# Rearranging the first pairs of batch 1 and the hand-over to batch 2 in a fused attention and expert kernel

## The chip, the cores and the metric

The kernel runs on one core of a Trainium2 chip. The metric is the device time of one execution in microseconds (us): the median of several runs. The profile is one execution, recorded by the hardware profiler. The engines are TensorE (PE in the profile: matrix products; PEld: its weight loads), VectorE (DVE), ScalarE (ACT), GpSimd (POOL) and SyncE (SP, which only issues transfers). [...]

## What is computed

Attention over 8 batches of 8 heads, 576 tokens and head width 64, in which a token sees the tokens within 32 places of it, and 8 "global" tokens see and are seen by all. Its output, as 4608 rows of 512, then goes through an expert layer with a squared Relu:

```python
scores = scale * q @ k.T                    # scale = 1/8
mask   = |pos_i - pos_j| <= 32  or  i global  or  j global
attn   = softmax(where(mask, scores, -1e9))
x      = (attn @ v)  as rows (batch, token), columns (head, width)   # 4608 x 512
h      = x @ w_in                           # 512 x 2048
out    = relu(h)**2 @ w_out                 # 2048 x 512, float32
```

## The kernel before

The attention of a batch is done in four pairs of heads (`hp`), the expert layer in nine chunks of 512 rows. The expert work is cut into units that stand in a list `queue`; `take(n)` emits the next n of them. The attention of one pair is laid between such units, so that TensorE has something to do while ScalarE and VectorE work on the pair.

```python
def take(n):
    for _ in range(min(n, len(queue))):
        fn, a = queue.pop(0)
        fn(*a)

def mm1_half(u, half, ...):        # chunk 0, first product, in two halves of 256 rows: 8 units each
    ...                            # 8 matmuls into one of three "mm" banks, then:
    rl = sbt("rl", [P, TC], FP16, bufs=3)...
    if u % 8 == 6:
        nc.vector.tensor_scalar(out=rl, in0=ph, ..., op0=ALU.max)
    else:
        nc.scalar.activation(out=rl, in_=ph, func=AF.Relu)
    nc.vector.tensor_tensor(out=gts[0][...], in0=rl, in1=rl, op=ALU.mult)
```

The other units are `mm1` (a column block of a later chunk: four matmuls of 512 columns, Relu, squaring) and `mm2` (four of the sixteen matmuls of 512 columns that make 128 output rows; the last one also copies the rows out of PSUM and stores them).

Batches 0 and 1 come in by token and are transposed on TensorE. Keys are copied out of PSUM by VectorE, queries by ScalarE:

```python
def tr_k(i, op=None, tail=None, last=None, tag="mm"):
    op = op or dve.tensor_copy
    tk, gl = transposed("k", i, tag)              # TensorE
    op(out=kt[:, 0:4, 8:P]..., in_=tk[:, 0:80]...)
    (tail or op)(out=kt[:, 4, 8 : 8 + KN[4]]..., in_=tk[:, 80:96])
    (last or op)(out=kt[:, :, 0:NG], in_=gl...)   # the global keys
```

`tr_q` does the same for queries in two copies. The rows of the global tokens' values are put ahead of each of the five key tiles:

```python
def v_globals(b, rows):
    dve.tensor_copy(out=gv16, in_=rows)
    for x in range(NT):                           # NT = 5
        dve.tensor_copy(out=vb[b][0:NG, x, 0 : 2 * H : 2], in_=gv16)
```

The start of the kernel:

```python
cast_tokens(dve.tensor_copy, "k", 0)
cast_tokens(dve.tensor_copy, "q", 0)
transposes0(0)                                    # tr_k(0), then tr_q(0)
cast_tokens(dve.tensor_copy, "k", 1)
cast_tokens(act.copy, "q", 1)
mask_natural(0)                                   # VectorE
keep_warm(SCHED["w3"])                            # filler: matmuls of a constant tile
tr_k(1, tail=act.copy, last=act.copy)
mg = mask_globals_matmul(0)                       # TensorE, reads the mask
keep_warm(SCHED["w4"])
tr_q(1, act.copy)
mask_globals(mg, 0)
...
```

From the end of batch 0 to batch 2. `scatter` writes the global tokens' outputs into their columns of `xT`, in eight copies on VectorE; chunk 0's second half reads them.

```python
tr_k(NHP, tag="tr")                               # NHP = 4: the first pair of batch 1
tr_q(NHP, tag="mm", op=act.copy)
scatter(0, 1)
v_globals(1, grow["v"][:, 0])
take(99)                                          # what is left of chunk 0's first half
queue += units[1] + units[2]                      # 8 + 16 units

def unit(i, n, nxt=None):
    scs = [scores(i, half, pair_tag[half], WIN2) for half in range(2)]   # TensorE
    et = [weights(half, scs[half], WIN2) for half in range(2)]           # exp on ScalarE, mask on VectorE
    take(n[0])
    if nxt:
        tr_k(nxt, tag="tr", tail=act.copy)
        tr_q(nxt, tag="mm", op=act.copy)
    for half in range(2):
        acc = outputs(i, half, et[half], ...)                            # TensorE
        finish_outputs(i, half, acc, ...)          # ln and exp on ScalarE, scaling on VectorE
        if half == 0:
            take(n[1])
    if i % NHP == NHP - 1:
        scatter(i // NHP)
    take(n[2])

for hp in range(NHP):
    unit(NHP + hp, SCHED["b1"][hp], NHP + hp + 1 if hp + 1 < NHP else None)   # (2, 1, 3) each
    if hp == 0:
        next_in_place()         # VectorE casts batch 2's global rows of k, q, v
        globals_to_scratch(2)   # SyncE: those rows of k and q into a scratch in DRAM
        pool.tensor_copy(out=pin[0:1], ...)
        tokens_to_scratch(2)    # GpSimd: the tokens of k and q into it, cast on the way
        transposes(2)           # SyncE: DMA transposes, scratch -> kb, qb
        vb[2] = vb[0]
        values(2)               # GpSimd: values, cast on the way
        value_globals(2)        # SyncE: global rows of the values
    if hp == 2:
        clear_ones(dve.memset, vb[0])
        index_base()
gather_index()
gather(0)
for b in range(2, B):
    queue += units[b + 1]
    for hp in range(NHP):
        unit(NHP * b + hp, ((2, 1, 4), (3, 1, 4), (2, 1, 5), (2, 1, 6))[hp])
        ...                     # at hp == 0: the same transfers for batch b + 1
    take(99)
queue += units[B + 1] + units[B + 2]
take(999)
```

Of the kernel before, what the change touches and what calls it, by code (L numbers as in the profile page):

```python
# [9 lines left out]
FP16 = mybir.dt.float16  # L10
# [8 lines left out]
NT = 5  # L19
# [20 lines left out]
)  # L40
W2 = 440
MB = (0, 456)
SCHED = dict(w5=2, w6=1, w7=2, wa=4, wb=3, wc=3, w0=6, w1=5, w2=2, w3=4, w4=0, w=4, h0=1, h1=1, h2=3, h3=0, b1=((2, 1, 3), (2, 1, 3), (2, 1, 3), (2, 1, 3)))
ONES = 2.0**-7 * (1.0 + 15360.0 / 2**23)


# [1 line left out]
def kernel(  # L48
# [29 lines left out]
    def sbt(name, shape, dtype, bufs=1, tag=None):  # L78
        return sb.tile(shape, dtype, name=name, tag=(tag or name), bufs=bufs)
# [260 lines left out]
    def store_rows(nm, b):  # L340
        gscr[(nm, b)] = dram.tile([NG, H * D], FP16, name=f"gscr_{nm}{b}")
        nc.sync.dma_start(
            out=gscr[(nm, b)].rearrange("g (h d) -> (g h) d", d=D), in_=gathered(nm, b)
        )
# [29 lines left out]
    def globals_to_scratch(b):  # L374
        for nm in "kq":
            rows, n, pitch, off = {"k": (KW, NT, P, 0), "q": (QW, 4, GRP, GTOK)}[nm]
            if (nm, b % 2) not in scr:
                scr[(nm, b % 2)] = dram.tile([rows, H * D], FP16, name=f"scr_{nm}{b % 2}")
                if nm == "k":
                    nc.sync.dma_start(  # L380
                        out=scr[("k", b % 2)][(NT - 1) * P + 8 + KN[-1] : KW],
                        in_=idle[0 : P - 8 - KN[-1]],
                    )
            t = scr[(nm, b % 2)]
            dst = t.rearrange("(x r) (h d) -> x r h d", x=n, d=D)[:, off : off + NG]
            if b == 2:
                nc.sync.dma_start(
                    out=dst.rearrange("x g h d -> g x (h d)"),
                    in_=g16s[nm].rearrange("g h d -> g (h d)").unsqueeze(1).to_broadcast(
                        (NG, n, H * D)  # L390
                    ),
                )
                continue
            nc.sync.dma_start(
                out=dst.rearrange("x g h d -> (g h) x d"),
                in_=gathered(nm, b).unsqueeze(1).to_broadcast((NG * H, n, D)),
            )
        if b > 2:
            store_rows("v", b)

    def tokens_to_scratch(b):
        for nm in "kq":
# [36 lines left out]

    gv16 = sbt("gv16", [NG, H, D], FP16)  # L440

    def v_globals(b, rows):
        dve.tensor_copy(out=gv16, in_=rows)
        for x in range(NT):
            dve.tensor_copy(out=vb[b][0:NG, x, 0 : 2 * H : 2], in_=gv16)

    def transposed(nm, i, tag):
        b, hp = divmod(i, NHP)
# [23 lines left out]
                    )  # L472
        return tr[:, 0:S].rearrange("p (j q) -> p q j", j=TJ), gl

    def tr_k(i, op=None, tail=None, last=None, tag="mm"):
        op = op or dve.tensor_copy
        tk, gl = transposed("k", i, tag)
        kt = kts[i % NHP]
        op(
            out=kt[:, 0:4, 8:P].rearrange("p t (q j) -> p t q j", j=TJ),  # L480
            in_=tk[:, 0:80].rearrange("p (t q) j -> p t q j", t=4),
        )
        (tail or op)(
            out=kt[:, 4, 8 : 8 + KN[4]].rearrange("p (q j) -> p q j", j=TJ), in_=tk[:, 80:96]
        )
        (last or op)(out=kt[:, :, 0:NG], in_=gl.unsqueeze(1).to_broadcast((P, NT, NG)))

    def tr_q(i, op=None, tag="mm"):
        op = op or dve.tensor_copy
        tq, gl = transposed("q", i, tag)  # L490
        q4 = qts[i % NHP].rearrange("p (g x) -> p g x", x=GRP)
        op(
            out=q4[:, :, 0:GTOK].rearrange("p g (q j) -> p g q j", j=TJ),
            in_=tq.rearrange("p (g q) j -> p g q j", g=4),
        )
        op(out=q4[:, :, GTOK:GRP], in_=gl.unsqueeze(1).to_broadcast((P, 4, NG)))
# [8 lines left out]
    def mm1(c, u):  # L505
        if c not in gts:
            gts[c] = sbt("gt", [P, NFF, TC], FP16, bufs=2)
        ph = expert_bank() if c else pst("mm", [P, 512])
        for t in range(NDM):
            nc.tensor.matmul(  # L510
                ph, w_in[:, t, u * P : (u + 1) * P], xT[:, t, XOFF + c * TC : XOFF + (c + 1) * TC],
                start=(t == 0), stop=(t == NDM - 1),
            )
        rl = sbt("rl", [P, TC], FP16, bufs=3)
        nc.scalar.activation(out=rl, in_=ph, func=AF.Relu)  # L515
        nc.vector.tensor_tensor(out=gts[c][:, u, :], in0=rl, in1=rl, op=ALU.mult)  # L516

# [2 lines left out]
    def mm1_half(u, half, tiles=range(NDM)):  # L520

        if 0 not in gts:
            gts[0] = sbt("gt", [P, NFF, TC], FP16, bufs=2)
        if 0 in tiles:
            ph_now[u] = pst("mm", [P, 2, 256])
        ph = ph_now[u]
        for j in range(2):
            for t in tiles:
                nc.tensor.matmul(
                    ph[:, j], w_in[:, t, (u + j) * P : (u + j + 1) * P],  # L530
                    xT[:, t, half * (256 + XOFF) : half * (256 + XOFF) + 256],
                    start=(t == 0 and j == 0), stop=(t == NDM - 1), skip_group_check=True,
                )
        if NDM - 1 not in tiles:
            return
        rl = sbt("rl", [P, TC], FP16, bufs=3).rearrange("p (j x) -> p j x", j=2)
        if u % 8 == 6:
            nc.vector.tensor_scalar(out=rl, in0=ph, scalar1=0.0, scalar2=None, op0=ALU.max)
        else:
            nc.scalar.activation(out=rl, in_=ph, func=AF.Relu)  # L540
        nc.vector.tensor_tensor(  # L541
            out=gts[0][:, u : u + 2, half * 256 : half * 256 + 256], in0=rl, in1=rl, op=ALU.mult
        )
# [192 lines left out]
    wv = moe_w_in.rearrange("(t p) f -> p t f", p=P)  # L736
    wo = moe_w_out.rearrange("(t p) m -> p t m", p=P)

    def transposes0(hp):
        tr_k(hp, tail=act.copy, last=act.copy)  # L740
        tr_q(hp, act.copy)

    keep_warm(SCHED["w0"])
    gb = indices()
# [2 lines left out]
    constants()  # L747
    one_hots(gb)
    cast_tokens(dve.tensor_copy, "k", 0)
    cast_tokens(dve.tensor_copy, "q", 0)  # L750
    transposes0(0)
    cast_tokens(dve.tensor_copy, "k", 1)
    cast_tokens(act.copy, "q", 1)
    mask_natural(0)
    keep_warm(SCHED["w3"])
    tr_k(1, tail=act.copy, last=act.copy)
    mg = mask_globals_matmul(0)
    keep_warm(SCHED["w4"])
    tr_q(1, act.copy)
    mask_globals(mg, 0)  # L760
    ets = {}

# [29 lines left out]
        fetch_values(1, x)  # L792
    for j in range(4):
        pool.dma_start(out=w_out[:, ts(j, 4), :], in_=wo[:, ts(j, 4), :])
    v_globals(0, gv0)
    half0(2)
    keep_warm(SCHED["w6"])
    half0(3)
# [36 lines left out]
    tr_k(NHP, tag="tr")  # L835
    tr_q(NHP, tag="mm", op=act.copy)
    scatter(0, 1)
    v_globals(1, grow["v"][:, 0])
    take(99)
    queue += units[1] + units[2]  # L840

    def unit(i, n, nxt=None):
        scs = [scores(i, half, pair_tag[half], WIN2) for half in range(2)]
        et = [weights(half, scs[half], WIN2) for half in range(2)]
        take(n[0])
        if nxt:
            tr_k(nxt, tag="tr", tail=act.copy)
            tr_q(nxt, tag="mm", op=act.copy)
        for half in range(2):
            acc = outputs(i, half, et[half], pair_tag[half], WIN2, columns=i < 2 * NHP)  # L850
            finish_outputs(i, half, acc, columns=i < 2 * NHP)
            if half == 0:
                take(n[1])
        if i % NHP == NHP - 1:
            scatter(i // NHP)
        take(n[2])

    for hp in range(NHP):
        unit(NHP + hp, SCHED["b1"][hp], NHP + hp + 1 if hp + 1 < NHP else None)
        if hp == 0:  # L860
            next_in_place()
            globals_to_scratch(2)
            pool.tensor_copy(out=pin[0:1], in_=xT[0:1, 0, XOFF + 256 : XOFF + 257])
            tokens_to_scratch(2)
            transposes(2)
            vb[2] = vb[0]
            values(2)
            value_globals(2)
        if hp == 2:
            clear_ones(dve.memset, vb[0])  # L870
            index_base()
    gather_index()
    gather(0)
    for b in range(2, B):
        queue += units[b + 1]
        for hp in range(NHP):
            unit(NHP * b + hp, ((2, 1, 4), (3, 1, 4), (2, 1, 5), (2, 1, 6))[hp])
            if b == 2 and hp:
                clear_ones(dve.memset, vb[1], range(2 * hp - 2, min(2 * hp, NT)))
            if hp == 0 and b + 1 < B:  # L880
                pool.tensor_copy(out=pin[0:1], in_=gsum[b][0:1, 0, 0, 0, 0:1])  # L881
                globals_to_scratch(b + 1)
                tokens_to_scratch(b + 1)
                transposes(b + 1)
                vb[b + 1] = vb[(b + 1) % 2]
                values(b + 1)
                value_globals(b + 1)
                if b in (2, 4):
                    gather(b // 2)
        take(99)  # L890
# [32 lines left out]
```

## Time and profile before

| what | value |
|---|---|
| time, median of 3 runs | 331.21 us (330.42 to 332.45) |
| span of the profiled execution | 329.3 us, granted TensorE clock 1.00 |
| TensorE busy | 316.9 us, 96% |
| VectorE busy | 231.1 us, 70% |
| ScalarE busy | 210.2 us, 64% |
| GpSimd busy | 106.5 us, 32% |
| TensorE, VectorE, ScalarE busy in the 10 us from 30 us | 7.98, 8.73, 7.10 us |
| the same, 40 to 50 us | 8.34, 8.46, 5.97 us |
| the same, 50 to 60 us | 9.59, 6.60, 5.50 us |
| the same, 60 to 70 us | 9.71, 8.36, 4.35 us |

"Busy" is the time in which an engine has an instruction running; TensorE's filler matmuls at the start count as busy too. A line of a timeline gives the start and the length of a group of like instructions in us, the engine, the line of the program, the operation, what it writes and reads, and in brackets how long the engine was idle before it and which instruction ended that. L529 are the matmuls of chunk 0's halves, L510 and L573 those of the later units, L458 the transposes, L613 the scores, L649 and L658 the outputs.

### The profile page before, as it was taken

What the parts mean: (1) busy time and instruction counts of PE and PEld (TensorE: products, weight loads), DVE (VectorE), ACT (ScalarE), POOL (GpSimd) and SP (SyncE); (2) the same over time, 40 slices, a digit from 0 to 9 for tenths busy, and PEclk for the clock granted to TensorE, in tenths of its full rate; (3) what the DMA queues carried; (4) which work ended last, traced back from release to release, by engine and by line L of the source; (5) the groups of instructions that cost most, each with busy time, mean ns of one, the idle gap of its engine ahead of it and who ended that gap; (6) DMA issues with size and microseconds to landing.
All of it is one profiled execution on the core that took longest, in us unless ns stands there. A gap on an engine that the chain in (4) does not pass through costs nothing.

```text
span 329.3 us, 6919 instructions
## 1 busy us (share of the span) xinstructions
PE 316.9 (96%) x2427; PEld 164.9 (50%) x2427; DVE 231.1 (70%) x684; ACT 210.2 (64%) x416; POOL 106.5 (32%) x138
## 2 busy tenths in 40 slices
PE   8889699999999999999999999999999999999996
PEld 3657574545554555455545554455454544444444
DVE  6896987788769775988588858885888584323421
ACT  2879574469954995499549954995499537404700
POOL 9734645019920770079207800680000000000000
PEclk9999999999999999999999999999999999999999
DMA  8999999949999999399959994999610001011012
GB/s 190 176 204 183 178 180 147 162 141 78 142 141 168 73 145 169 109 96 144 124 143 100 135 149 118 115 148 120 128 66 0 34 33 64 2 64 64 2 49 78
DMA packets 148356, 37.55 MB, mean 114 GB/s; under 512 B 136298, under 2 KB 143842, under 8 KB 148322
## 3 DMA queue, kind: packets, MB, share of 16 engines
q0 software_dynamic: 105168, 17.93, 77.1%
q1 hardware_dynamic: 43008, 19.05, 30.7%
q8 instruction: 19, 0.31, 0.4%
q14 instruction: 15, 0.12, 0.1%
q10 hardware_dynamic: 146, 0.13, 0.1%
HBM read 37.31 MB, written 17.05 MB: 165 GB/s over the span
## 4 chain that ended last, share of the span: by engine, by line
PE 78%; DVE 11%; ACT 5%; issue 2%; DMA 2%; SPq 2%; DVEq 0%
PE mm L573 25%; PE mm L510 25%; PE tr L510 9%; PE tr L573 6%; PE sc L658 3%; PE acc L658 3%; PE sc L613 2%; DVE xT L730 2%; ACT rec L682 2%; SPq L357 2%; ACT rec L681 2%; PE acc L613 2%; DMA grows<-in_k_dram 1%; DVE xT L711 1%; DVE gt L541 1%
## 5 line engine op out<-in xcount | busy, mean ns | idle before, releaser
L573 PE MATMUL mm<-w_out,gt 128*128 128x512 f16 x448 | 104.4, 379 | 0.0
L510 PE MATMUL mm<-xT,w_in 128*128 128x512 f16 x384 | 90.1, 379 | 0.8 <-DVE xT L730 0.8
L573 PEld LDWEIGHTS <-gt 128*128 128x128 f16 x560 | 52.5, 98 | 58.6
L510 PEld LDWEIGHTS <-w_in 128*128 128x128 f16 x512 | 47.5, 98 | 53.9 <-issue 1.0
L515 ACT ACTIVATE rl<-mm 128x512 f16<-128x512 f32 x96 | 54.9, 599 | 25.9 <-PE mm L510 25.3
L516 DVE TENSOR_TENSOR gt<-rl 128x512 f16<-128x512 f16 x128 | 52.0, 423 | 16.7 <-ACT rl L515 14.6
L622 ACT ACTIVATE et<-sc 128x880 f16<-128x880 f32 (+1 forms) x32 | 28.9, 902 | 44.7 <-PE sc L613 44.7
L625 DVE TENSOR_TENSOR et<-et,mask 128x880 f16<-128x880 f16 (+1 forms) x64 | 38.7, 613 | 22.4 <-ACT et L622 22.1
L113 POOL DMA_DIRECT2D vb<-in_v_dram x40 | 40.7, 1551 | 8.3 <-DMA w_in<-in_moe_w_in_dram 7.1
L510 PE MATMUL tr<-xT,w_in 128*128 128x512 f16 x128 | 33.0, 380 | 0.0
L550 DVE COPY ot<-mm 128x512 f32<-128x512 f32 (+1 forms) x29 | 19.7, 679 | 17.5 <-PE mm L573 15.8
L711 DVE TENSOR_TENSOR xT<-sc,rec 64x288 f16<-64x288 f32 (+1 forms) x55 | 25.0, 455 | 7.2 <-ACT rec L682 6.9
L682 ACT ACTIVATE rec<-rec 128x288 f32<-128x288 f32 x64 | 28.3, 443 | 2.0
L622 ACT ACTIVATE et<-acc 128x880 f16<-128x880 f32 (+1 forms) x32 | 29.0, 905 | 0.0
L658 PEld LDWEIGHTS <-vb 128*128 128x128 f16 x288 | 21.2, 98 | 12.9 <-issue 2.1
L711 DVE TENSOR_TENSOR xT<-acc,rec 64x288 f16<-64x288 f32 (+1 forms) x55 | 25.0, 455 | 3.7 <-ACT rec L682 0.9
L406 POOL DMA_DIRECT2D scr_k<-in_k_dram x30 | 26.5, 1084 | 2.5 <-issue 2.0
L406 POOL DMA_DIRECT2D scr_q<-in_q_dram x24 | 24.8, 1553 | 4.9 <-DMA w_out<-in_moe_w_out_dram 4.9
L681 ACT ACTIVATE rec<-sc 64x288 f32<-64x288 f32 (+1 forms) x55 | 22.4, 407 | 6.1 <-PE sc L658 4.2
L573 PE MATMUL tr<-w_out,gt 128*128 128x512 f16 x112 | 25.3, 379 | 0.0
L881 POOL COPY pin<-gsh 1x1 f32<-1x1 f32 x5 | 0.9, 185 | 70.9 <-DVE gsh L699 70.9
L681 ACT ACTIVATE rec<-acc 64x288 f32<-64x288 f32 (+1 forms) x55 | 22.2, 404 | 1.5 <-PE acc L649 0.6
(143 smaller groups left out, 302.1 us busy)
## 6 DMA issues: line engine op xcount, KB each, us to landing
out_dram<-ot SPq DMA_DIRECT2D x35, 256.0 KB
vb<-in_v_dram POOLq DMA_DIRECT2D x32, 120.0 KB, 10.7
scr_q<-in_q_dram POOLq DMA_DIRECT2D x24, 144.0 KB, 5.7
scr_k<-in_k_dram POOLq DMA_DIRECT2D x24, 120.0 KB, 4.6
w_in<-in_moe_w_in_dram POOLq DMA_DIRECT2D x4, 512.0 KB, 11.4
w_out<-in_moe_w_out_dram POOLq DMA_DIRECT2D x4, 512.0 KB, 12.5
natk<-in_k_dram POOLq DMA_DIRECT2D x3, 288.0 KB, 14.4
natq<-in_q_dram POOLq DMA_DIRECT2D x3, 288.0 KB, 15.1
```

The costliest lines, as they stand in the source:

```text
L113: pool.dma_start(out=vb[b][NG : NG + KN[x], x, 2 * hs.start : 2 * hs.stop : 2], in_=v[b, hs, x * KT : x * KT + KN[x]].rearrange("h s d -> ...
L406: pool.dma_start(out=scr[(nm, b % 2)][x * pitch + off : x * pitch + off + hi - lo].rearrange("s (h d) -> s h d", d=D), in_=src[nm][b, :, l ...
L510: nc.tensor.matmul(ph, w_in[:, t, u * P : (u + 1) * P], xT[:, t, XOFF + c * TC : XOFF + (c + 1) * TC], start=(t == 0), stop=(t == NDM - 1),)
L515: nc.scalar.activation(out=rl, in_=ph, func=AF.Relu)
L516: nc.vector.tensor_tensor(out=gts[c][:, u, :], in0=rl, in1=rl, op=ALU.mult)
L573: nc.tensor.matmul(po, gts[c][:, f, m * P : (m + 1) * P], w_out[:, f, :], start=(f == 0), stop=(f == NFF - 1),)
L622: act.activation(out=et[:, :, 0:W], in_=sc[:, :, 0:W], func=AF.Exp, bias=0.0, scale=scale)
L625: dve.tensor_tensor(out=et[:, :, 0:W], in0=et[:, :, 0:W], in1=mask[:, MB[half] : MB[half] + W].unsqueeze(1).to_broadcast((P, 2, W)), op=AL ...
L658: nc.tensor.matmul(banks[e][:, o : o + w], vtf[:, t, vo : vo + P], et[:, e, so : so + w], start=(n == 0), stop=(n == nw - 1), skip_group_c ...
L681: act.activation(out=rec[r], in_=av[xs][rs, :, 0:GTOK], func=AF.Ln)
L682: act.activation(out=rec, in_=rec, func=AF.Exp, scale=-1.0)
L711: dve.tensor_tensor(out=xT[r, hp, x0 : x0 + HS].rearrange("p (k x) -> p k x", k=2), in0=av[x][r, :, 0:GTOK], in1=rec[r], op=ALU.mult,)
```

## The change

The change spreads the work around the first pair of batch 1 over more engines, keeps an expert unit in hand for the places where TensorE has nothing else, and does the preparation of batch 2 in smaller pieces. Part by part:

1. **Start.** The first pair's queries are cast on ScalarE in place of VectorE. In both pairs the query copies come ahead of the key tails on ScalarE. The second pair's key transposes come after the mask's matmul.
2. **First pair of batch 1.** Of chunk 0's first half one unit is held back (`keep=1`) until the pair's scores are out, and the pair takes three units there in place of two. The value rows' cast goes to ScalarE, and of the five copies two; VectorE does three, after the pair's weights.
3. **Query copy ahead of key tail** in the other pairs of batch 1 too.
4. **Relu of chunk 0's halves.** Four `rl` buffers in place of three; VectorE does the Relu of units (0, 6), (1, 4) and (1, 12), where it did (0, 6), (0, 14), (1, 6) and (1, 14).
5. **Batch 2's rows.** The cast of its global rows, their way to the scratch, the transposes and the value rows come after the second pair of batch 1, where they came after the first. The token transfers and the values stay after the first. The scratch tensors are made there.
6. **Small VectorE work.** The ones of batch 2's values are set in two pieces, after the weights of the third and the fourth pair; the index arithmetic and the gather of later batches' rows go to the third pair.
7. **Units per pair.** Batch 1's last pair takes two at its end in place of three, so that one unit is left over for batch 2's first pair; the last batch takes one less in its third pair and one more after its scatter.

```diff
-SCHED = dict(..., h3=0, b1=((2, 1, 3), (2, 1, 3), (2, 1, 3), (2, 1, 3)))
+SCHED = dict(..., h3=0, keep=1, b1=((3, 1, 3), (2, 1, 3), (2, 1, 3), (2, 1, 2)), last=((2, 1, 4), (3, 1, 4), (2, 1, 4), (2, 1, 7)))
 ...
-    def v_globals(b, rows):
-        dve.tensor_copy(out=gv16, in_=rows)
-        for x in range(NT):
-            dve.tensor_copy(out=vb[b][0:NG, x, 0 : 2 * H : 2], in_=gv16)
+    def spread_values(b, op, tiles=range(NT)):
+        for x in tiles:
+            op(out=vb[b][0:NG, x, 0 : 2 * H : 2], in_=gv16)
 ...
     def tr_k(..., then=None):
         op(out=kt[:, 0:4, 8:P]..., in_=tk[:, 0:80]...)
+        if then:
+            then()
         (tail or op)(...)
 ...
-        rl = sbt("rl", [P, TC], FP16, bufs=3)...
-        if u % 8 == 6:
+        rl = sbt("rl", [P, TC], FP16, bufs=4)...
+        if (half, u) in ((0, 6), (1, 4), (1, 12)):
 ...
     cast_tokens(dve.tensor_copy, "k", 0)
-    cast_tokens(dve.tensor_copy, "q", 0)
-    transposes0(0)
+    cast_tokens(act.copy, "q", 0)
+    tr_k(0, tail=act.copy, last=act.copy, then=lambda: tr_q(0, act.copy))
 ...
-    tr_k(1, tail=act.copy, last=act.copy)
     mg = mask_globals_matmul(0)
     keep_warm(SCHED["w4"])
-    tr_q(1, act.copy)
+    tr_k(1, tail=act.copy, last=act.copy, then=lambda: tr_q(1, act.copy))
 ...
-    v_globals(1, grow["v"][:, 0])
-    take(99)
+    take(len(queue) - SCHED["keep"])
+    act.copy(out=gv16, in_=grow["v"][:, 0])
     queue += units[1] + units[2]
 
-    def unit(i, n, nxt=None):
+    def unit(i, n, nxt=None, then=None):
         scs = ...
         et = ...
+        if then:
+            then()
         take(n[0])
+        if i == NHP:
+            spread_values(1, act.copy, range(3, NT))
         if nxt:
-            tr_k(nxt, tag="tr", tail=act.copy)
-            tr_q(nxt, tag="mm", op=act.copy)
+            tr_k(nxt, tag="tr", tail=act.copy, then=lambda: tr_q(nxt, tag="mm", op=act.copy))
         for half in range(2):
             ...
             if half == 0:
                 take(n[1])
+                if i == NHP + 2:
+                    index_base()
+                    gather_index()
 ...
+    def between(hp):
+        if hp == 0:
+            spread_values(1, dve.tensor_copy, range(0, 3))
+        elif hp == 2:
+            clear_ones(dve.memset, vb[0], range(0, 2))
+        elif hp == 3:
+            clear_ones(dve.memset, vb[0], range(2, NT))
 
     for hp in range(NHP):
-        unit(NHP + hp, SCHED["b1"][hp], ...)
+        unit(NHP + hp, SCHED["b1"][hp], ..., lambda: between(hp))
         if hp == 0:
+            for i in range(2):
+                make_scratch(i)
+            pool.tensor_copy(out=pin[0:1], ...)
+            tokens_to_scratch(2)
+            vb[2] = vb[0]
+            values(2)
+        elif hp == 1:
             next_in_place()
             globals_to_scratch(2)
-            pool.tensor_copy(out=pin[0:1], ...)
-            tokens_to_scratch(2)
             transposes(2)
-            vb[2] = vb[0]
-            values(2)
             value_globals(2)
-        if hp == 2:
-            clear_ones(dve.memset, vb[0])
-            index_base()
-    gather_index()
-    gather(0)
+        elif hp == 2:
+            gather(0)
     for b in range(2, B):
         queue += units[b + 1]
         for hp in range(NHP):
-            unit(NHP * b + hp, ((2, 1, 4), (3, 1, 4), (2, 1, 5), (2, 1, 6))[hp])
+            n = ((2, 1, 4), (3, 1, 4), (2, 1, 5), (2, 1, 6)) if b < B - 1 else SCHED["last"]
+            unit(NHP * b + hp, n[hp])
```

## The prediction

> **What bounds the kernel now.** I read the page first, then TensorE's timeline and waits over the stretch the change touches, then the timelines of VectorE and of SyncE's queue there. The page's engine row:
>
> ```profile
> PE 316.9 (96%) x2427; PEld 164.9 (50%) x2427; DVE 231.1 (70%) x684; ACT 210.2 (64%) x416; POOL 106.5 (32%) x138
> ```
>
> TensorE (PE) is the bound: 329.3 - 316.9 = 12.4 us without a matmul. Up to 25 us part of its "busy" is filler (matmuls of `idle`), so the start is a chain of latencies; from 75 to 260 us it hardly stops. What real work there is to regain is in its gaps from 34 to 75 us. TensorE's timeline (start, length, instruction; in brackets the idle time before it and what ended it):
>
> ```profile
> 34.75 0.36 PE L613 MATMUL sc<-qt,kt 64*128 64x160 f16 x6
> ...
> 36.01 1.92 PE L529 MATMUL mm<-xT,w_in 128*128 128x256 f16 x16 [0.71 <-DVE xT L730]
> 37.86 0.45 PE L458 MATMUL tr<-identity,natk 96*64 96x96 f16 x12
> 39.63 0.45 PE L458 MATMUL mm<-identity,natq 96*64 96x96 f16 x12 [1.31 <-ACT rl L540]
> 40.86 0.26 PE L649 MATMUL sc<-et,vb 128*64 128x160 f16 x2 [0.78 <-DVE et L625]
> ...
> 49.78 0.26 PE L649 MATMUL sc<-et,vb 128*64 128x160 f16 x2 [0.84 <-DVE et L625]
> ...
> 55.23 0.37 PE L613 MATMUL acc<-qt,kt 64*128 64x112 f16 x6 [0.41 <-DVE xT L711]
> ...
> 65.23 0.26 PE L649 MATMUL sc<-et,vb 128*64 128x160 f16 x2 [0.29 <-DVE et L625]
> ...
> 71.00 1.89 PE L510 MATMUL mm<-xT,w_in 128*128 128x512 f16 x8 [0.53 <-DVE xT L730]
> ```
>
> Seven waits: 0.71 + 1.31 + 0.78 + 0.84 + 0.41 + 0.29 + 0.53 = 4.87 us; one more of 0.25 us comes at 270 us, before chunk 7, behind the last batch's scatter. All but the second name VectorE, and the second is VectorE's too, as its own timeline shows:
>
> ```profile
> 34.11 1.84 DVE L730 COPY xT<-gx 128x4 f16 x8
> 36.15 0.41 DVE L443 CAST gv<-grows 8x512 f16<-8x512 f32 x1 [0.20 <-issue]
> 36.60 1.96 DVE L445 COPY vb<-gv 8x512 f16<-8x512 f16 x5
> 38.49 0.74 DVE L541 TENSOR_TENSOR gt<-rl 128x512 f16<-128x512 f16 x2
> 39.15 0.67 DVE L538 TENSOR_SCALAR rl<-mm 128x512 f16<-128x512 f32 x1
> 39.86 0.42 DVE L541 TENSOR_TENSOR gt<-rl 128x512 f16<-128x512 f16 x1
> 40.20 1.14 DVE L625 TENSOR_TENSOR et<-et,mask 128x880 f16<-128x880 f16 x2
> ```
>
> Scatter and value rows keep it 4.4 us. Behind them stand the squarings (which free the three `rl`), the Relu of unit 14 (which frees the `mm` bank that the query transposes want) and the weights of the pair.
>
> The other side is the way of batch 2's rows, on SyncE's queue, whose instructions block one another:
>
> ```profile
> 48.10 0.28 SPq L387 DMA_DIRECT2D scr_k<-g16sk  x1
> 48.90 0.28 SPq L387 DMA_DIRECT2D scr_q<-g16sq  x1
> 52.86 5.37 SPq L418 DMA_TRANSPOSE kb<-scr_k  x1
> 58.46 6.15 SPq L418 DMA_TRANSPOSE qb<-scr_q  x1
> 64.72 3.97 SPq L427 DMA_DIRECT2D vb<-g16sv  x5
> ```
>
> The queue's waits give this as the last before `kb`:
>
> ```profile
> SPq L418 <- DMA scr_k<-g16sk: 1.1, 1, 1.1
> ```
>
> So the key transpose starts when the cast rows have landed, 4.76 us after their issue. In the packet records the two transposes' 4,992 packets run from 55.3 to 66.3 us; batch 2's scores need them at 69.91 us. That is slack now, about 3 us.
>
> [...] the Relu waits for its turn until 39.15 us and TensorE does not pass over the blocked transpose. [...] the rows' 4.76 us fall while GpSimd's casting transfers move about 1,150 packets per us, whereas the output stores issued at 68.74 us move about 1 us later. [...] an 8x512 cast takes 0.62 us on ScalarE (L368) against 0.41, so the split buys parallelism, not cheaper work.
>
> **The change, part by part.**
>
> *Prologue.* The first query cast (0.98 us) leaves VectorE for ScalarE (0.85 for the second one). Little comes of it: the first key transposes at 6.03 us stand behind filler, and VectorE's next copy waits for them. But the mask matmul (8.70 to 9.08) now precedes the second pair's key transposes (8.21 before), and it needs the mask rows that VectorE finishes at about 8.85. The key copy at 8.89 slips to about 9.55. VectorE waits for global rows at 15.33 us with 0.26 us to spare, and 0.66 less some idle time on the way is about 0.5: a loss of about 0.3 us.
>
> *First pair of batch 1.* With one unit held back, its scores come one unit (8 matmuls, 0.93 us) earlier, but not before the key copy ends (34.2). VectorE's order becomes scatter to 35.95, two squarings to 36.65, weights 2 x 0.55 to 37.75, three value copies at about 0.36 to 38.8. The rest goes to ScalarE, idle 36.9 to 39.0 now: Relu of unit 14 to 37.4, two more to 38.6, two value copies at about 0.6 (estimated from L368) to 39.8. Four `rl` and the Relu on ScalarE remove the 1.31 wait. TensorE: units still wait for scatter at 36.0, transposes to 38.6, first outputs 38.75 instead of 40.86: 2.1 us.
>
> *Second and third pair.* VectorE has lost the row casts (1.26 us, moved on), a Relu (0.67), the value cast (0.41) and two copies (0.78) ahead of 49.20. Query copy ahead of key tail lets ScalarE copy queries while VectorE copies keys, taking up to 0.74 us (0.54 + 0.20) out of its chain to the logarithms. That covers 0.84 and 0.41: the gain is about 3.4 at 55 us. Index arithmetic, 1.8 us of small VectorE instructions, now sits in the third pair before its second outputs are scaled; I give back 0.35 there. Clearing the ones after the weights takes the 0.29 away. With the prologue's 0.3, TensorE comes to batch 2's scores at about 65.8 us, with one unit (0.86 us of 512-column matmuls) still queued: in work done, 69.91 - 65.8 - 0.86 = 3.25 us ahead. That unit covers most of the 0.53; scatter ends at about 67.7, so (1, 0) of chunk 1 can start no sooner than that: 71.0 - 67.7 = 3.3 us.
>
> *Batch 2's rows.* The key-row cast falls behind the second pair's output copy, at about 52.9 us instead of 48.07. The rows land 4.0 us on (less traffic): key transpose at about 56.9. From there to the last query packet it took 14.1 us (52.86 to about 67) beside value transfers that land until about 64.5. These finish sooner with nothing competing, so the second half runs freer: after them 1,490 packets took 1.3 us. I choose 10.5 us, between 8.5 and 13: landing at 67.4. TensorE then waits 1.6 us at scores, and chunk 1 starts at 67.4 + 0.5 + 0.86 = 68.8 instead of 71.0: 2.2 us stay.
>
> *Later.* The last batch's shifted unit covers the 0.25. Batch 3's transfers start earlier, but nothing waits for them now (no TensorE wait between 75 and 260 us). The `last` counts otherwise reorder the same 32 units.
>
> Sum: 331.2 - 2.2 - 0.25 = 328.8 us.
>
> **Rivals.** (1) *The rows become the wait that ends last.* For: from the row cast TensorE has only about 13 us of work to the scores; landing and transposes took 19 us before. Against: much of that 19 was traffic that will be over. If the transposes keep 14 us, they land at 71, scores then start later than before, and the time is 331.5 to 332. (2) *No such wait:* transposes take 8.5 us, all 3.5 us stay: 327.6. (3) *ScalarE becomes the chain.* It takes the value cast, two copies and a Relu, 2.4 us more in the first pair, just before the query copy. For: the copies are strided and 0.6 is an estimate. Against: 2.1 us of idle lay there. With 1 us each, the second outputs wait 0.5: 329.3. (4) *The prologue costs more:* if the mask matmul holds both pairs' chains, 0.7 us instead of 0.3: 329.2.
>
> **Range and chances.** 326.9 has rival 2 with no prologue loss; 331.2 has rival 1 in its mild form. More than 2% either way is 6.6 us: all gaps the change can reach sum to 5.1, and a loss would need the transposes some 9 us later than I reckon. So 0.03 faster, 0.95 within, 0.02 slower.
>
> **What would show it.** In the changed profile: no wait for `rl` before the query transposes of the first pair, first outputs near 38.8 us; no wait near 47; rows issued near 53 and the key transpose near 57; TensorE idle 1 to 2 us before batch 2's first scores, ended by a DMA or SyncE; no wait at 270. I am wrong if that wait is absent or over 3 us, if a wait on ScalarE's value copies appears, or if the first global value cast comes later than 15.9 us.

## The result, and the profile after

The changed kernel takes 327.26 us against 331.66 us for the kernel before beside it; the ratio is 0.9869 (95% interval 0.9824 to 0.9915). In a second comparison, with more executions, it is 327.29 us against 331.27 us, ratio 0.9897 (0.9865 to 0.9930). So about 4 us, or 1.0 to 1.3%, are gained.

The page of the first profile of the changed kernel, engine row and granted clock of TensorE in 40 slices of 8.2 us:

```profile
PE 318.2 (97%) x2427; PEld 166.8 (51%) x2427; DVE 228.5 (70%) x679; ACT 212.8 (65%) x421; POOL 106.7 (33%) x138
...
PEclk9669999999999999999999999999999999999999
```

The clock row holds what no step of the prediction has: from 11.3 to 21.6 us TensorE ran at half its clock. The span of this profile is 326.4 us, 2.9 less than before. A second profile of the same kernel, called "the second profile" below, has the full clock throughout and a span of 324.2 us. I read the steps there, because the kernel before had the full clock too. TensorE's timeline in it, first pair of batch 1 and then batch 2's first scores:

```profile
34.16 0.36 PE L614 MATMUL sc<-qt,kt 64*128 64x160 f16 x6 [0.30 <-DVE kt L487]
...
35.89 1.92 PE L530 MATMUL mm<-xT,w_in 128*128 128x256 f16 x16 [0.19 <-DVE xT L731]
...
38.02 0.43 PE L457 MATMUL mm<-identity,natq 96*64 96x96 f16 x12
38.29 0.24 PE L650 MATMUL sc<-et,vb 128*64 128x160 f16 x2
...
66.10 0.37 PE L614 MATMUL sc<-qb,kb 64*128 64x160 f16 x6 [0.82 <-DVE xT L731]
...
67.46 1.03 PE L511 MATMUL mm<-xT,w_in 128*128 128x512 f16 x4
```

The waits of 1.31 and 0.78 us are gone: the query transposes follow at 38.02 us and the first outputs at 38.29 us, where they stood at 39.63 and 40.86. Chunk 1 begins at 67.46 us, where it began at 71.00. The reason is VectorE's queue in the second profile:

```profile
34.02 1.81 DVE L731 COPY xT<-gx 128x4 f16 x8
35.73 0.75 DVE L542 TENSOR_TENSOR gt<-rl 128x512 f16<-128x512 f16 x2
36.40 1.14 DVE L626 TENSOR_TENSOR et<-et,mask 128x880 f16<-128x880 f16 x2
37.45 1.18 DVE L444 COPY vb<-gv 8x512 f16<-8x512 f16 x3
```

The weights (L626) now follow at 36.40 us; before they came at 40.20. Batch 2's rows on SyncE's queue, in the second profile, then in the first, and below it TensorE's line in the first:

```profile
52.24 0.28 SPq L380 DMA_DIRECT2D scr_k<-g16sk  x1
...
57.78 2.87 SPq L418 DMA_TRANSPOSE kb<-scr_k  x1
60.89 2.63 SPq L418 DMA_TRANSPOSE qb<-scr_q  x1
```

```profile
54.72 0.28 SPq L380 DMA_DIRECT2D scr_k<-g16sk  x1
...
60.20 2.88 SPq L418 DMA_TRANSPOSE kb<-scr_k  x1
63.33 2.57 SPq L418 DMA_TRANSPOSE qb<-scr_q  x1
```

```profile
68.41 0.37 PE L614 MATMUL sc<-qb,kb 64*128 64x160 f16 x6 [0.99 <-DMA qb<-scr_q]
```

In the first profile the two transposes hold SyncE's queue for 2.88 and 2.57 us, where they held it for 5.37 and 6.15. They run when most of the value transfers are over: from 60 to 64 us no packet of GpSimd's queue starts there, while in the kernel before, beside its transposes, 164 to 1,293 of them start in each microsecond from 53 to 62 us. The query transpose does end the wait before batch 2's scores there. The second profile names VectorE's scatter for the same wait of 0.82 us, but the last packets of the query transpose start at 65.2 us there, 0.9 us before the scores; in the first profile they start at 67.5, also 0.9 before. So I take it to be the transpose in both.

The times of all kernels that ran, with the span and the mean clock of their profiles:

| kernel | median us | ratio to before | 95% interval | span us | clock |
|---|---|---|---|---|---|
| changed, first comparison | 327.26 | 0.9869 | 0.9824 to 0.9915 | 326.4 | 0.983 |
| changed, second | 327.29 | 0.9897 | 0.9865 to 0.9930 | 324.2 | 1.000 |
| changed, mask matmul last | 327.27 | 0.9896 | 0.9861 to 0.9931 | 324.3 | 1.000 |
| before, mask matmul first | 331.69 | 1.0013 | 0.9997 to 1.0029 | 330.0 | 0.995 |
| changed, rows after first pair | 329.41 | 0.9938 | 0.9916 to 0.9960 | 327.7 | 0.995 |
| changed, value rows on VectorE | 328.25 | 0.9893 | 0.9850 to 0.9937 | 327.1 | 0.984 |
| changed, key tail first | 327.55 | 0.9899 | 0.9846 to 0.9952 | 325.6 | 1.000 |
| changed, no unit held back | 327.04 | 0.9891 | 0.9833 to 0.9949 | 323.8 | 1.000 |
| changed, old Relu and three `rl` | 327.92 | 0.9896 | 0.9854 to 0.9938 | 325.8 | 1.000 |
| before, four `rl` | 330.68 | 0.9977 | 0.9946 to 1.0009 | 328.5 | 1.000 |
| changed, values late | 331.24 | 0.9988 | 0.9967 to 1.0009 | 330.5 | 0.990 |
| changed, old numbers of units | 326.64 | 0.9852 | 0.9836 to 0.9869 | 324.6 | 1.000 |
| changed, no filler before the mask | 328.50 | 0.9892 | 0.9858 to 0.9927 | 326.2 | 0.979 |

Half a per cent can't be told apart by the medians. So the experiments are read by landmarks in the profiles: the start of each pair's exp on ScalarE, in kernels that ran at the full clock up to there. Numbers such as "1.4 us later" below mean that. A landmark has its own scatter. Five profiles at full clock whose program is the same up to batch 1's first pair (the second profile, rows after first pair, values late, old numbers of units, key tail first) have that pair's exp between 34.91 and 35.67 us. So a difference of less than 0.8 us at one landmark shows nothing by itself; what is gained or lost between two landmarks shows more.

### The profile page after: what moved, and what is told of

Read it like the earlier page. It is cut to its first block, busy times and chain, and to the rows that moved or that the text cites. A ratio compares the mean times of both kernels' runs of the same rounds, so it can differ in the third digit from the quotient of the medians.

```text
span 326.4 us, 6931 instructions
## 1 busy us (share of the span) xinstructions
PE 318.2 (97%) x2427; PEld 166.8 (51%) x2427; DVE 228.5 (70%) x679; ACT 212.8 (65%) x421; POOL 106.7 (33%) x138
## 4 chain that ended last, share of the span: by engine, by line
PE 86%; DVE 6%; DMA 3%; ACT 3%; issue 1%; SPq 0%; DVEq 0%
PE mm L574 27%; PE mm L511 26%; PE tr L511 9%; PE tr L574 7%; PE sc L659 3%; PE acc L659 3%; PE sc L614 2%; PE acc L614 2%; PE mm L530 2%; DMA stk<-in_k_dram 2%; DMA qb<-scr_q 2%; DVE xT L731 1%; ACT rec L683 1%; PE mm L457 1%; DVE xT L712 1%
## 5 line engine op out<-in xcount | busy, mean ns | idle before, releaser
L517 DVE TENSOR_TENSOR gt<-rl 128x512 f16<-128x512 f16 x128 | 51.1, 423 | 16.6 <-ACT rl L516 15.4
L626 DVE TENSOR_TENSOR et<-et,mask 128x880 f16<-128x880 f16 (+1 forms) x64 | 39.1, 615 | 22.9 <-ACT et L623 22.6
## 6 DMA issues: line engine op xcount, KB each, us to landing
vb<-in_v_dram POOLq DMA_DIRECT2D x32, 120.0 KB, 10.5
```

What stands on the lines that cost most here:

```text
L626: dve.tensor_tensor(out=et[:, :, 0:W], in0=et[:, :, 0:W], in1=mask[:, MB[half] : MB[half] + W].unsqueeze(1).to_broadcast((P, 2, W)), op=AL ...
```

## The experiments

### The control

> The changed kernel once more, as a control. Theory (idle gap): the mask matmul put ahead leaves TensorE idle for about 1.3 us near 7.4 us, and that gap is what let the granted clock fall to a half for 10.24 us in the first profile; where the fall comes, the first chunk-0 unit starts near 27.1 us and the span is near 326.4, where it does not, near 25 us and 324.5. Rival (chance): the fall has nothing to do with the gap. Both expect 326 to 328 us here; the gap near 7.4 us is there in any case.

Median 327.29 us. The clock was full, and the gap on TensorE before the mask matmul only 0.41 us, not the 1.3 that was expected in any case. The clock records show the full clock from 4.5 us in the first profile and from 6.9 here; the five filler matmuls from 4.00 us took 1.47 us there and 2.31 here, and the four right ahead of the gap started at 6.33 and at 7.22 us. The mask matmul came at 8.66 and 8.65 us.

### The mask matmul put last again

```diff
-    mg = mask_globals_matmul(0)
     tr_k(1, ..., then=lambda: tr_q(1, act.copy))
+    mg = mask_globals_matmul(0)
```

> The changed kernel with the mask matmul behind the second pair's transposes again. Idle-gap theory: no gap over 0.5 us near 8 us, clock 1.00 in the start, first chunk-0 unit at 24.3 to 24.7 us, and 1 to 2 us faster than the changed kernel (325 to 326 us). Chance rival: same time as the changed kernel within 0.6 us, and the clock falls as often. Rival (rows bind): the start is gained, but batch 2's query transpose then ends the wait before the scores, so that wait grows from 1.0 to 2 us or more and less than 1 us is kept.

Median 327.27 us, the same as the changed kernel; the 1 to 2 us that the idle-gap theory expected did not come. The profile has the full clock, but a gap of 0.82 us on TensorE before the query transposes, where none over 0.5 was expected. So the order neither gains nor loses in the median. One of its eight executions has a mean clock of 0.983, which is what the first profile's 10.24 us at half clock gave, so about as much half clock came with this order too, wherever in the execution it lay. The first pair's exp is 0.5 us earlier than in the second profile (10.78 against 11.29 us), and at batch 1's first pair both are level (35.04 and 35.12): the 0.5 us of the start are lost on the way.

### The kernel before with the mask matmul first

```diff
-    tr_k(1, tail=act.copy, last=act.copy)
     mg = mask_globals_matmul(0)
+    tr_k(1, tail=act.copy, last=act.copy)
     tr_q(1, act.copy)
```

> The kernel before with only the mask matmul moved ahead of the second pair's key transposes. Idle-gap theory: a gap of about 1 us on TensorE before the mask matmul; the first chunk-0 unit, at 24.58 us before, comes 0.3 to 0.9 us later with a full clock and 2.5 us later with a fallen one; time 331.5 to 334. Chance rival: 0.3 us later, full clock, time within 0.5 us of before.

Median 331.69 us, ratio 1.0013, not told apart from before. The first pair's exp comes 0.74 us later, the third pair's 0.57, batch 1's first pair's 0.17: most of the delay is lost ahead of the expert layer. A stretch of 3.41 us at half clock begins at 40.5 us, after that kernel's wait of 1.31 us and within the next, of 0.8; it leaves the kernel 0.74 us behind from there on.

### Batch 2's rows back after the first pair

```diff
             values(2)
+            next_in_place()
+            globals_to_scratch(2)
+            transposes(2)
+            value_globals(2)
         elif hp == 1:
-            next_in_place()
-            globals_to_scratch(2)
-            transposes(2)
-            value_globals(2)
```

> The changed kernel with the cast of batch 2's rows, their way to the scratch, the transposes and the value rows after the first pair again. Theory: the row cast (1.3 us) stands before the second pair's weights, so TensorE waits 0.3 to 0.8 us before that pair's first outputs; the query transpose ends 1 to 2.5 us earlier, so the wait of 0.99 us before batch 2's scores goes; the two about cancel: within 0.7 us of the changed kernel. Rival (the shift is what pays): 1 us or more slower than the changed kernel, with waits of over 1 us in the second pair. Rival (the shift costs): 1 us faster.

Median 329.41 us: 2.1 us slower than the changed kernel, so the rival holds that the shift is what pays. But not for the reason that either gives. In the second pair TensorE waits only 0.13 us for the weights. The large wait is the one before batch 2's scores, which was expected to go:

```profile
45.53 0.28 SPq L380 DMA_DIRECT2D scr_k<-g16sk  x1
...
51.76 6.02 SPq L418 DMA_TRANSPOSE kb<-scr_k  x1
58.01 7.05 SPq L418 DMA_TRANSPOSE qb<-scr_q  x1
```

```profile
68.09 0.37 PE L614 MATMUL sc<-qb,kb 64*128 64x160 f16 x6 [2.50 <-DMA qb<-scr_q]
```

The rows are issued 6.7 us sooner than in the second profile (52.24 us), the key transpose starts 6.0 us sooner, and batch 2's scores can begin 2.0 us later; 0.55 us of that was there at batch 1's first pair, before anything that the edit moves. Beside the value transfers the transposes take 6.02 and 7.05 us of SyncE's queue.

Much of the 2.1 us goes with the clock. The profile has 3.41 us at half clock behind the wait, and the distance to the second profile grows there from 2.0 to 3.7 us. Of the 22 executions the six with a mean clock of 0.999 and more have a median of 327.83 us, against 327.23 for five such executions of the changed kernel; the 16 others have 329.77.

### Value transfers held back

```diff
-            values(2)                       # after the first pair
         ...
         elif hp == 2:
+            pool.tensor_copy(out=pin[0:1], in_=xT[0:1, 2, XOFF + S : XOFF + S + 1])
+            values(2)
             gather(0)
```

> The changed kernel with the transfers of batch 2's values held back until the third pair of batch 1. Theory (the value traffic is what makes the rows and the transposes slow): the rows land 2.5 to 4 us after their issue in place of 5.5, the key transpose starts at 54.5 to 56.5 us in place of 57.8, the query transpose ends before TensorE comes to batch 2's scores, and the wait of 0.8 to 1.0 us there goes; as scatter ends about then too, 0.3 to 0.6 us of it is kept. Rival (the queue's own pace): the rows still take 5 us and more, the wait stays. Rival (values become the last to land): a new wait of 1 us or more before batch 2's first outputs, and the kernel is slower.

Median 331.24 us; the profile's wait at the scores is 5.38 us, and 6.83 us of half clock begin within it. The queue shows the theory in its first half and its failure in the second:

```profile
52.67 0.28 SPq L380 DMA_DIRECT2D scr_k<-g16sk  x1
...
56.18 2.87 SPq L418 DMA_TRANSPOSE kb<-scr_k  x1
59.28 4.86 SPq L418 DMA_TRANSPOSE qb<-scr_q  x1
```

```profile
70.61 0.55 PE L614 MATMUL sc<-qb,kb 64*128 64x160 f16 x6 [5.38 <-DMA qb<-scr_q]
```

Without value traffic the rows need 3.5 us from issue to the key transpose (5.5 in the second profile), and the key transpose 2.87. At 57.9 us the values start, and the query transpose takes 4.86 in place of 2.63; its last packets start at 68.2 us, against 65.2. The scores come 2.4 us after them and not 0.9, which these records don't explain. The later start of the same traffic made the query transpose late. So in these runs a transpose's time on the queue goes with the value traffic beside it: 2.87 us without, 4.86 with it here, 6.02 and 7.05 with the rows after the first pair. The packets show it from one microsecond to the next too: from 58 to 60 us 685 and then 1,091 of this kernel's transpose packets start in a microsecond, with none from GpSimd's queue; from 62 to 67 us it is 359 to 452, beside 146 to 398 of that queue. Why they share the time so, these runs don't show.

### The value rows back on VectorE

```diff
+    dve.tensor_copy(out=gv16, in_=grow["v"][:, 0])
+    spread_values(1, dve.tensor_copy)
     take(len(queue) - SCHED["keep"])
-    act.copy(out=gv16, in_=grow["v"][:, 0])
 ...
-        if i == NHP:
-            spread_values(1, act.copy, range(3, NT))
 ...
-        if hp == 0:
-            spread_values(1, dve.tensor_copy, range(0, 3))
```

> The changed kernel with the value rows' cast and all five copies on VectorE again, ahead of the squarings as before. Theory (VectorE's queue was the bound of the first pair): weights 2.0 to 2.4 us later, TensorE waits 1 to 2 us before the first pair's first outputs, exp of the second pair 1 to 2 us later than in the changed kernel; later gaps take some of it up (the wait of about 0.8 us before batch 2's scores does not, as the row cast slips too), so 0.7 to 1.7 us slower. Rival (four rl buffers and the moved Relu alone removed the first pair's waits): within 0.5 us.

Median 328.25 us, 1.0 us more than the changed kernel's. Its profile has the same half clock in the start as the first profile (11.4 to 21.7 us), so it is compared with that one: at the first pair's exp 37.12 against 37.48 us, at the second pair's 47.89 against 46.40. The first outputs wait:

```profile
42.07 0.26 PE L650 MATMUL sc<-et,vb 128*64 128x160 f16 x2 [1.23 <-DVE et L626]
```

From 0.36 us ahead to 1.49 behind, 1.85 us go in the one pair. By batch 2's second pair the distance is 0.8 us (77.19 against 76.41): the wait before batch 2's scores shrank to 0.19 us, and took up part, which I had not expected.

### Key tail ahead of query copy

```diff
-            tr_k(nxt, tag="tr", tail=act.copy, then=lambda: tr_q(nxt, tag="mm", op=act.copy))
+            tr_k(nxt, tag="tr", tail=act.copy)
+            tr_q(nxt, tag="mm", op=act.copy)
```

> The changed kernel with the key tail ahead of the query copy in the pairs of batch 1. Theory: the logarithm of each pair's first half starts 0.5 to 0.7 us later, and TensorE's small waits before the next pair's second scores grow by 0.3 to 0.6 us in two of three pairs: 0.4 to 1.0 us slower. Rival: ScalarE has room by now, under 0.3 us.

Median 327.55 us; by landmarks 1.36 us later at the second pair, 1.5 at the fourth, 1.64 at batch 2's second pair. But 0.43 us of this are there at the first pair's exp, before anything that the edit moves. So the edit costs 0.9 to 1.2 us in this profile, at the upper end of what was expected or a little over. TensorE's waits in the stretch:

```profile
43.76 1.03 PE L530 MATMUL mm<-xT,w_in 128*128 128x256 f16 x8 [0.74 <-DVE rl L539]
...
61.20 0.37 PE L614 MATMUL acc<-qt,kt 64*128 64x112 f16 x6 [0.87 <-DVE xT L712]
```

The first is for the Relu of unit (1, 4), which stands in VectorE's queue behind the first half's scaling, which waits for ScalarE. The order of two copies on ScalarE comes to TensorE by way of VectorE.

### No unit held back

```diff
-SCHED = dict(..., keep=1, b1=((3, 1, 3), ...
+SCHED = dict(..., keep=0, b1=((2, 1, 3), ...
```

> The changed kernel with no unit held back (first pair 2, 1, 3). The first pair's exp was at 35.16 us before and 35.12 us in the changed kernel, so theory: holding back only swaps a wait of 0.7 us for scatter against one of 0.3 us for the key copy and 0.2 for scatter; 0 to 0.4 us slower. Rival (the change is named after it): 0.9 us slower, one whole unit.

Median 327.04 us. The wait for scatter is 0.73 us, as before, in place of 0.30 and 0.19; the first pair's exp is at 35.14 us (35.12 with the unit held back), the second's 0.3 us sooner. But this profile was 0.8 us ahead at batch 0's last pair, where the two programs are still the same. So the landmarks don't show whether holding back gains; the medians show no gain.

### The old Relu and three buffers; four buffers alone

```diff
-        rl = sbt("rl", [P, TC], FP16, bufs=4)
-        if (half, u) in ((0, 6), (1, 4), (1, 12)):
+        rl = sbt("rl", [P, TC], FP16, bufs=3)
+        if u % 8 == 6:
```

> The changed kernel with three rl buffers and the Relu of units (0, 6), (0, 14), (1, 6), (1, 14) on VectorE. Theory: with the value rows off VectorE's queue the Relu of (0, 14) comes at once, so the wait of 1.31 us before the query transposes comes back only in part (0 to 0.6 us): 0 to 0.6 us slower. Rival: it comes back whole, over 1 us slower.

Median 327.92 us. At batch 2's second pair it is 0.73 us later, a little over the expected range; then it falls back by another 0.85 us, to 1.58 at batch 7's second pair, where nothing but the number of `rl` buffers differs from the changed kernel. Hence the converse, the kernel before with four:

```diff
-        rl = sbt("rl", [P, TC], FP16, bufs=3)
+        rl = sbt("rl", [P, TC], FP16, bufs=4)
```

> The kernel before with four rl buffers in place of three and nothing else. The profiles so far fall in two groups: from batch 3 to batch 7 the kernels with three buffers keep step with one another, and those with four do, but the second group gains about 0.9 to 1.0 us on the first, some 0.18 us in each batch's first pair. Theory (the fourth buffer does it): the exp of the last pair comes 1.2 to 2.5 us before 261.53 us, 0.9 to 1.0 us of it gained after 104 us, and part of the wait of 1.31 us in the first pair goes; time 0.8 to 2.2 us less. Rival (something else in the change does it): no gain after 104 us.

Median 330.68 us, ratio 0.9977 (0.9946 to 1.0009). From batch 3's first pair to batch 7's third it gains 0.9 us on the kernel before (from 0.06 behind to 0.83 ahead): 0.15 in batch 3's second pair and 0.18 in the first pair of each later batch. Its only edit is the buffer, so the fourth buffer does gain in the later batches. In the first pair of batch 1 it alone gains nothing:

```profile
40.90 0.26 PE L649 MATMUL sc<-et,vb 128*64 128x160 f16 x2 [2.29 <-DVE et L625]
```

The wait of 1.31 us for the bank is gone, and the next one grew from 0.78 to 2.29, to the same moment (40.86 before). The queue behind scatter and value rows was the cause; the buffer was only where it first showed.

### The old numbers of units

```diff
-b1=((3, 1, 3), (2, 1, 3), (2, 1, 3), (2, 1, 2)), last=((2, 1, 4), (3, 1, 4), (2, 1, 4), (2, 1, 7))
+b1=((3, 1, 3), (2, 1, 3), (2, 1, 3), (2, 1, 3)), last=((2, 1, 4), (3, 1, 4), (2, 1, 5), (2, 1, 6))
```

> The changed kernel with the old numbers of units in batch 1's last pair and in the last batch, so that none is left over for batch 2's first pair and none stands behind the last scatter. Theory: TensorE comes to batch 2's scores 0.86 us later, so the wait for the query transpose nearly goes, and then waits 0.3 to 0.8 us for scatter before chunk 1; at 268 us a wait of 0.2 to 0.3 us comes back: 0.3 to 0.7 us slower in all. Rival: a whole unit, 0.9 us or more slower.

Median 326.64 us, the lowest of all, though its interval overlaps the changed kernel's; span 324.6 against 324.2 us. The waits:

```profile
66.77 0.37 PE L614 MATMUL sc<-qb,kb 64*128 64x160 f16 x6 [1.24 <-DMA qb<-scr_q]
...
265.86 2.75 PE L511 MATMUL mm<-xT,w_in 128*128 128x512 f16 x12 [0.26 <-DVE xT L731]
```

The wait of 0.26 us at the last scatter comes back, as expected. The one before batch 2's scores didn't shrink, and none for scatter before chunk 1 appeared: the scores came 0.7 us later in this profile although the rows were issued 0.5 us sooner. The key transpose starts 0.7 us sooner too, but the two hold the queue for 3.82 and 3.15 us, not 2.87 and 2.63, and why is not shown. By spans the unit's place is worth 0.4 us; the medians show none of it.

### No filler before the mask matmul

```diff
-SCHED = dict(..., w3=4, ...
+SCHED = dict(..., w3=0, ...
```

> The changed kernel without the four filler matmuls between the first pair's transposes and the mask matmul, so that TensorE is idle there for 1.4 to 2.3 us whatever the start looks like. So far the clock was halved from about 11.4 to 21.6 us in both profiles of this order whose gap was 1.30 us, and in none of the profiles whose gap was 0.2 to 0.8 us. Theory [...]: a half clock in the profile between 10 and 22 us, first chunk-0 unit near 27 us in place of 24.5, time 1.5 to 2.5 us more than the changed kernel. Rival (chance): clock 1.00 there, time within 0.7 us.

Median 328.50 us, 1.2 more than the changed kernel, a little under the expected range; the interval of its ratio overlaps. The profile has the half clock that the theory expected:

```profile
PEclk9569999999999999999999999999999999999999
```

```profile
7.95 0.40 PE L262 MATMUL acc<-mask,oh 128*8 128x160 f16 x3 [1.29 <-DVE mask L245]
```

The clock is at half from 8.7 to 22.4 us. Chunk 0's first unit comes 2.9 us later than in the second profile (27.38 against 24.49), and 2.0 us of that are left at the end. Six of the seven executions have a mean clock of 0.978 to 0.984; of the changed kernel's thirteen, two have 0.983 and 0.984.

## Why the prediction was right, and where it was wrong

The measured 327.26 us lies inside 326.9 to 331.2, close to its lower end; 328.8 was 1.5 us too high. The second profile against the profile before, step by step, with the scatter of 0.8 us to be kept in mind:

| step | predicted | measured |
|---|---|---|
| prologue | 0.3 us lost | first chunk-0 unit 24.58 before, 24.49 after; 23.71 to 25.27 in six profiles with the same start at full clock |
| first outputs of the first pair | 38.75 us, 2.1 gained | 38.29 us, 2.6 gained |
| gain at the third pair | 3.4 us | 3.5 us (exp 54.86, then 51.32) |
| row issue | 52.9 us | 52.24 us |
| issue to key transpose | 4.0 us | 5.5 us |
| key transpose to batch 2's scores | 10.5 us | 8.3 us |
| wait at batch 2's scores | 1.6 us | 0.8 us (1.0 in the first profile) |
| chunk 1 starts | 68.8 us | 67.46 us |
| batches 3 to 7 | nothing | 1.0 us gained |
| wait before chunk 7 | 0.25 us gone | gone |

*First pair: right.* VectorE's queue was the bound, as the second set of lines had it. Undoing the split costs 1.85 us in that pair, and four buffers alone only move the wait. "ScalarE becomes the chain" did not come: its two value copies take 1.12 us together, as estimated, and end in time.

*Second and third pair: the size right, the parts not.* The query copy ahead of the key tail was taken as up to 0.74 us of one chain; undone, it costs 0.9 to 1.2 us, since the Relu of (1, 4) stands behind it in VectorE's queue. The 0.35 us given back for the index arithmetic was 0.43 in the second profile. For the unit held back no gain is shown, and I had given it none of its own.

*Batch 2's rows: mechanism right, term mis-sized.* The step that failed is "I choose 10.5 us". From the start of the key transpose to the scores it is 8.3 us, just under the band of 8.5 to 13, because with most of the values landed the transposes run at nearly twice the pace. In the second profile their 4,992 packets of 256 bytes run from 59.2 to 65.2 us, which is 1.28 MB in 6.0 us, 215 GB/s; before, they ran from 55.0 to 66.0 us (the prediction read 55.3 to 66.3), 116 GB/s. From 61 to 62 us, in the second profile, 1,128 packets start, 289 GB/s. The rows' landing went the other way (5.5 us, not 4.0): when they were issued, the values were still on the way. The two errors partly cancel: 4.0 + 10.5 = 14.5 us were predicted from the issue to the scores, and 13.9 came. Over the nine profiles with this order of transfers the two terms are 3.9 to 5.5 and 8.2 to 9.8 us.

*Rival 1 came true in small.* The rows do end the wait there, by 0.8 to 1.0 us. What I called the cost of the shift was its gain: with the rows after the first pair the wait is 2.5 us. The lines of the kernel before that I used, 5.37 and 6.15 us on the queue, already held this: I took from them that the traffic slows the transposes, but not that it nearly halves their pace (116 against 215 GB/s).

*"Nothing waits for them now (no TensorE wait between 75 and 260 us)": right as a reading, wrong as a reason for no gain.* In the profile of the kernel before, TensorE is busy in 184.88 of these 185 us. Yet a buffer that I had booked only in batch 1 gains 0.9 to 1.0 us there.

*Prologue: small at full clock, and blind to the clock.* Of a loss of half a microsecond at the first exp (11.29 against 10.85) nothing is to be seen by 24.5 us, where profiles of the same start differ by 1.6 us; so the 0.3 us is neither confirmed nor refuted. What I missed is that the same reordering opens a gap on TensorE: in the first profile it was 1.30 us, and the clock fell to half 2.65 us after its end, which took back about 2.5 us (first chunk-0 unit at 27.08 us).

Together, at full clock: 3.7 us at batch 3's first pair, 1.0 in batches 3 to 7 and about 0.3 at the end make 5.0 of the 5.1 us between the spans of 329.3 and 324.2 us. Predicted were 2.2, nothing and 0.25. The medians show 4.0 of this; the four executions of the first comparison had mean clocks of 0.983, 0.995, 0.999 and 0.998 with times of 328.21, 327.34, 326.16 and 327.18 us, so part of the rest is probably clock. Without the 1.0 us of the later batches, which no step had forecast, the time would have been about 328.3 us, close to the predicted 328.8.

## What to carry to other kernels

Before moving a late transfer forward, look at which other transfers run where it would go: here the two transposes took 6.02 and 7.05 us beside the value traffic and 2.87 and 2.63 after most of it, and starting 6 us later ended 1.4 to 2 us sooner. When a wait is for a buffer or a bank, ask who is slow in giving it back; a further buffer moved the wait from 1.31 + 0.78 to 2.29 us without any gain, while taking work off the slow queue removed it. And compare two kernels by landmarks along the whole span, not by listed waits alone: a microsecond came in five pieces that no list showed. Take the scatter of the landmarks first, from profiles of the same program.

## What was not expected of the hardware

**The clock fell to half behind one wait and not behind another of the same length.** TensorE's granted clock was 1.0 or 0.5 in the clock records and nothing between. Its stretches at half, but for those that run past the end of a span, lasted 3.41, 6.83, 10.24 and 13.65 us. In the start it was halved in the profiles whose gap before the mask matmul was 1.30, 1.30 and 1.29 us, and in none of the eleven others, where that gap, or the one that took its place, was at most 0.82 us. The first profile's line:

```profile
8.66 0.42 PE L262 MATMUL acc<-mask,oh 128*8 128x160 f16 x3 [1.30 <-DVE mask L245]
```

It came later too: 3.41 us behind the wait of 2.50 us, and 6.83 from within that of 5.38. Behind the same wait of 1.31 us it came in the kernel before with the mask matmul first, but not in the kernel before, and not behind the 2.29 of that kernel with four buffers. So the length of the wait alone does not decide in these profiles. What does, these runs don't show.

**What it costs** depends on the stretch: 10.24 us at half clock in the latency-bound start took about 2.5 us; 3.41 us took about 0.6 at 40.5 us (0.17 us behind before it, 0.74 after) and 1.7 at 68.7 us, with the rows after the first pair.

**Where the fourth buffer's 0.18 us per batch goes** inside the first pair is seen only in part. In batch 4's first pair TensorE's third output matmul comes 0.08 us sooner with four buffers, and the second pair's exp 0.18. That the number of buffers does it is shown; by which wait is not.
